# Strassen's products for half of h in two more chunks, and bursts of small matmuls moved by empty TensorE instructions

## The chip, the cores and the metric

The kernel runs on one NeuronCore of a Trainium2 chip. A core has TensorE (matmuls into PSUM), VectorE (DVE in the profile), ScalarE (ACT), GpSimd (POOL), SyncE (SP) and 16 DMA engines. The metric is the device time of one execution in microseconds, the median of several. The profile's span runs from the first to the last instruction of the program and is a little shorter than that time.

## The reference

Eight batches of eight heads pass through a linear attention with cosine weights; its output goes, token by token, through a two-layer network with a swish whose slope is a vector.

```python
# q, k, v: (8, 8, 576, 64); w_in: (512, 2048); w_out: (2048, 512); beta: (2048,)
q_p = concat(relu(q) * cos, relu(q) * sin)          # the same for k
kv  = einsum('bhsf,bhsd->bhfd', k_p, v)
z   = sum(k_p, axis=2)
num = einsum('bhsf,bhfd->bhsd', q_p, kv)
den = einsum('bhsf,bhf->bhs', q_p, z) + 1e-6
x   = num / den                                     # 4608 tokens x 512
h   = x @ w_in
out = (h * sigmoid(beta * h)) @ w_out               # 4608 x 512, float32
```

## The kernel before

The 4608 tokens are cut into nine chunks of 512 (c = 0 to 8). While chunk c passes through the network, the attention of batch b = c + 1 is done between its matmuls. All matmuls of the network are bfloat16.

**The first layer.** h of a chunk is 16 row tiles (jt) of 128 x 512. The plain way takes four matmuls of 128x512 for a tile:

```python
def h_mm(c, jt, mis=range(4), blocks=slice(0, NB)):
    ...
        nc.tensor.matmul(ps[:, h_bank(c, jt), ...], lhsT=win[jt // 4][:, mi, ...], rhs=xt[:, blocks, jp, ...], ...)

def h_plain(c, jt, bank, cols=1):       # the same; cols=2 cuts three of the four matmuls into two of 128x256
    w = NB // cols
    for mi in range(MI):
        for o in range(0, NB, w) if mi else (0,):
            ...
            nc.tensor.matmul(ps[:, bank, o * 64 : z * 64], lhsT=win[...], rhs=xt[:, o:z, jp, ...], ...)
```

From chunk FAST = 5 on, eight of the 16 tiles are done in four pairs (named X, Y, Z, V) by Strassen's scheme in Winograd's form: a pair is a product of 2 x 2 blocks that takes seven block products instead of eight. Each block product is two matmuls of 128x256, so a pair takes 14 of 128x256 where the plain way takes eight of 128x512. The operands that are sums of blocks are made on VectorE: four of the weights for each pair, once for all chunks (`wh_sums`), and four of x in each chunk (`x_sums`, or `x_sum` one at a time).

```python
def wh_sums(jt):                        # four TENSOR_TENSORs of 128x256
    ...
def x_sums(c):                          # four TENSOR_TENSORs of 128x512, from the chunk's x
    ...
def h_fast(c, jt0, banks):
    ops = {
        "1": lambda: prod(b_ps, w(0, 0), x(0, 0), True, False),   # prod: two matmuls of 128x256
        "5": lambda: prod(e_ps, s1, t1, True, False),
        "6": lambda: prod(b_ps, s2, t2, False, False),
        "2": ...  "7": ...  "3": ...  "4": ...
        "c1": lambda: nc.scalar.copy(p1, b_ps),                   # copies and additions between the products
        "c5": lambda: nc.vector.tensor_copy(p5, e_ps),
        "cu": ...  "a2": ...  "a7": ...  "a3": ...
        "Sa": ...  "Sb": ...                                      # SiLU of the two tiles
    }
```

**The second layer.** From chunk 2 on it is wholly done by the same scheme, in two halves x and y: seven products each, every one of eight matmuls of 128x256 (`o_fast`). Its sums over g (`g_sums`, tiles S1 to S4) are made on VectorE while h is computed. `cols` can cut a product's matmuls into two of 128x128.

**The attention.** Two groups of small matmuls of a batch come in bursts, without anything between them: `kv_mm` (72 matmuls of 64x130) and `num_all` (3 x 48 = 144 matmuls of 64x65). With the weight loads, the second is a burst of 288 TensorE instructions. VectorE then divides (`x_div`: sum, reciprocal and product, for a third of the batch each), and a DMA transposes the result into a chunk's x.

**The order in chunks 2 to 4 (before FAST).** `h_first` runs the 16 tiles plainly and puts the sums of VectorE between them; then the burst and the second layer:

```python
def h_first(c):
    for slot in range(16):
        h_group(c, slot)
        if c == 2: ...                             # k, v and q of the next batch on VectorE
        if slot == (10 if c == 2 else 1):
            kv_all(b)
        if slot in (3, 7, 11):
            g_sums(c, slot // 2 - 1, slot // 2 + 1)
        elif slot in (13, 15):
            sums = g_sums(c, slot // 2, slot // 2 + 1)
        if c == FAST - 1 and slot in (2, 4, 6, 8, 10, 12):
            wh_sums((0, 4, 8, 12, 2, 6)[slot // 2 - 1])

parts = (6, 0, 4) if c < FAST else (0, 6, 4)       # PSUM banks of the burst's thirds
xb, yb = (2, 3, 6), ...                            # banks of the second layer: b, e, a
...
sums = h_first(c)
for t, bank in enumerate(parts):
    num_all(b, t, bank)                            # the burst
for i, n in enumerate("156273"):
    x[n]()                                         # products 1, 5, 6, 2, 7, 3; product 2 writes bank 6
    if n in "156":
        ...
        x_part(b, i, parts[i])                     # x_div and the transpose
...                                                # the half y, with v of the next batch between
if c == FAST - 1:
    x_sums(c + 1)                                  # behind all v_half of VectorE
```

**From FAST on** one string gives the order of all operations: p0 to p7 are plain tiles, sp their SiLU, X5 a product of pair X, a2X an addition, s13 a sum of g, K and N the two bursts, ox5 a product of the second layer, v, w, k, q the next batch's preparation, t1 to t4 the sums of x for the next chunk. ORDER serves chunks 5 and 6, ORDER_END chunks 7 and 8. Two tables, H_COLS and O_COLS, cut matmuls of chunks 5 and 6 in two.

Of the kernel before, what the change touches and what calls it, by code (L numbers as in the profile page):

```python
# [22 lines left out]
def kernel(  # L23
# [172 lines left out]
    def q_relu(b, jp, eng="dve"):  # L196
        relu(qb[:, jp].rearrange("q n (j d) -> q j n d", j=2), raw_tile(b, "q")[:, 2 * jp : 2 * jp + 2], eng)
# [130 lines left out]
    def num_all(b, t, bank):  # L328
        for i in range(3):
            for jp in range(2):  # L330
                num_mm(b, 3 * t + i, jp, bank, 2 * i + jp)
# [82 lines left out]
    def h_silu(c, jt, bank):  # L414
        if (c, jt // 4) not in gs:
            gs[c, jt // 4] = gt_pool.tile([P, 4, TCH], BF16, name="g_t", tag="g_t")
        nc.scalar.activation(gs[c, jt // 4][:, jt % 4], ps[:, bank], AF.Silu, scale=beta[:, jt : jt + 1])  # L417

    def h_plain(c, jt, bank, cols=1):
        xt = xt_tile(c)  # L420
        w = NB // cols
        for mi in range(MI):
            jp, g = divmod(mi, 2)
            for o in range(0, NB, w) if mi else (0,):
                z = o + w if mi else NB
                nc.tensor.matmul(ps[:, bank, o * 64 : z * 64], lhsT=win[jt // 4][:, mi, (jt % 4) * P : (jt % 4 + 1) * P],  # L426
                                 rhs=xt[:, o:z, jp, g * HP : (g + 1) * HP],
                                 start=(mi == 0), stop=(mi == MI - 1 and z == NB))
# [101 lines left out]
    def o_part(c, tt, part, cols=1):  # L530
        o_mm(c, tt, range(4 * part, 4 * part + 4), cols)
# [226 lines left out]
    def v_half(b, cs, n0=0, n1=NQ, eng="dve"):  # L758
        if b >= B:
            return  # L760
        v_scale(b, cs, n0=n0, n1=n1, eng=eng)
        if cs == 1 and n1 == NQ and b + 1 < B:
            load_raw(b + 1, "v")
# [65 lines left out]
    for slot in range(32):  # L829
        if slot < 16:  # L830
            h_group(1, slot)
        else:
            o_part(1, (slot - 16) // 4, slot % 4, 2 if slot > 23 else 1)
        one_unit(slot)

    def k_piece(b, j):
# [4 lines left out]
            load_raw(b + 1, "k")  # L841

    ORDER = (
        "Y1 c1Y X5 X1 c5X c1X p0 X6 Y6 cuX X2 cuY X3 a2X a3X sp0 K X7 p1 kt Z1 Y5 a7X c5Y X4 SaX sp1 SbX "
        "Y7 a7Y s01 p2 Y2 s03 Z5 a2Y c1Z sp2 Y4 Y3 SbY Z6 Z2 a3Y SaY p4 V5 a2Z c5Z cuZ s02 c5V V1 p3 q0 "
        "sp4 Z7 V3 c1V V2 V6 a7Z Z3 sp3 Z4 cuV q1 p5 a3Z a2V SbZ V7 SaZ s11 s04 a3V a7V p6 sp5 s12 p7 "
        "sp6 s13 SaV V4 s21 s23 s14 SbV s22 N0 sp7 ox1 s31 ox5 s32 k1 x0 c1o s33 ox6 k0 k2 k3 c5o oy1 "
        "s24 ox2 s34 g0 g1 v8 w4 v4 x1 c1y o2x ox3 v2 v7 cuo x2 oy6 ox7 oy2 cuy o3x o7x oy5 oy7 ox4 w8 "
        "o2y v6 c5y t1 t3 oy3 w1 w0 o7y t2 v5 v3 oy4 t4 o3y w7 v1 w6 c4x w5 w3 w2 v0 c4y")
    ORDER_END = (  # L850
        "E1 F1 E2 X1 c1E X5 c1X X2 E5 a2E c5X X6 E6 X3 c1F a2X Y1 cuX X7 c5E cuE c1Y E3 E7 Y6 a3X SaX cuY "
        "a7X a3E Y5 SaE a7E X4 F6 F5 Y7 c5Y E4 Y2 cuF c5F Y3 F7 F2 a7Y a3Y a7F SbX SbE Y4 F3 a2Y Z1 a2F "
# [1 line left out]
        "V2 sp4 s13 sp5 V7 Z7 p6 a2V a3V s12 SaZ p7 SaV a7V sp6 sp7 a7Z s02 Z4 s14 V4 s04 oy1 SbV s31 SbZ "  # L854
        "s21 c1y s22 ox1 ox2 s32 t1 c1o ox5 o2x s34 s24 oy6 ox6 cuy cuo s23 oy2 s33 oy7 c5o ox3 ox7 o3x "
        "o7x oy5 c5y ox4 c4x t2 o7y oy3 t4 t3 o2y o3y oy4 c4y")
    H_COLS, O_COLS = {6: 8}, {5: ("4", "25734")}

    def x_sum(c, kind):
        xt, n = xt_tile(c), NB // 2  # L860
# [5 lines left out]
    def prep(b, left):  # L866

        def take(op):
            n = int(op[1])
            if op[0] in "kvw" and b + 1 < B:  # L870
                if op[0] == "k":
                    k_relu(b + 1, n, n + 1, "act")
                else:
                    v_scale(b + 1, "wv".index(op[0]), n0=n, n1=n + 1, eng="act" if op[0] == "v" else "dve")
            elif op[0] == "q" and b + 2 < B:
                q_relu(b + 2, n)
            for names, act in left:
                if names and op in names:
                    names.discard(op)
                    if not names:  # L880
                        act()

        return take

    def chunk(c, b, x, y, parts):
        steady = {"X": (0, 2, 0, 1), "Y": (4, 3, 4, 5), "Z": (8, 0, 2, 1), "V": (12, 4, 3, 5)}
        end = {"X": (0, 6, 0, 1), "E": (2, 5, 3, 4), "Y": (4, 2, 0, 1), "F": (6, 7, 3, 4), "Z": (8, 6, 0, 1),
               "V": (12, 5, 3, 4)}
        pairs = {n: h_fast(c, at[0], at[1:]) for n, at in (steady if b < B else end).items()}

        def plain_bank(n):
            return (2 if n == 7 else 6 + n % 2) if b < B else (2, 7)[n % 2]

        plain = [2, 3, 6, 7, 10, 11, 14, 15]
        outs = {"x": x, "y": y}

        def q_next():
            if b + 2 < B:
                q_turn_dma(b + 2)
                if b + 3 < B:  # L900
                    load_raw(b + 3, "q")

        def raw_next(name):
            if b + 2 < B:
                load_raw(b + 2, name)

        xs_all = {"x0", "x1", "x2"}
        take = prep(b, [
            ({"k0", "k1", "k2", "k3"} | xs_all, lambda: raw_next("k")),
            ({"q0", "q1"} | xs_all, q_next),  # L910
            ({f"{o}{n}" for o in "vw" for n in range(NQ)}, lambda: raw_next("v"))])
        last_sum = None
        for op in (ORDER if b < B else ORDER_END).split():
            n = int(op[-1]) if op[-1].isdigit() else None
            if op == "K":
                kv_mm(b, 0, 4)
                kv_mm(b, 1, 4)
            elif op == "kt":
                kv_take((0, 1), 4)
            elif op[0] == "N":  # L920
                for t, bank in enumerate(parts):
                    num_all(b, t, bank)
            elif op[0] == "x":
                x_part(b, n, parts[n])
                take(op)
            elif op[0] in "kvwq":
                take(op)
            elif op[0] == "t":
                if c + 1 < NTC:
                    x_sum(c + 1, n)  # L930
            elif op[0] == "g":
                if b + 1 < B:
                    q_tan(b + 1, n, None if n else last_sum)
            elif op[0] == "p":
                h_plain(c, plain[n], plain_bank(n), 2 if n < H_COLS.get(c, 0) else 1)
            elif op[:2] == "sp":
                h_silu(c, plain[n], plain_bank(n))
            elif op[0] == "o" and n is not None:
                outs[op[1]][op[2]]()
            elif op[0] == "o":  # L940
                outs[op[2]]["a" + op[1]]()
            elif op[0] == "c" and op[2] in "xyo":
                outs["x" if op[2] == "o" else op[2]][op[:2]]()
            elif op[0] == "s":
                last_sum = g_sum(c, 2 * int(op[1]), 2 * int(op[1]) + 2, n)
            else:
                pair = op[0] if op[0] in pairs else op[-1]
                pairs[pair][op.replace(pair, "")]()

    def h_first(c):  # L950
        b = c + 1
        for slot in range(16):
            h_group(c, slot)
            if c == 2:
                if slot == 0:
                    wx_tiles()
                    k_all(b)
                    v_half(b, 1)
                if slot == 3:
                    att_q(b + 1)  # L960
                if slot == 5:
                    nc.vector.tensor_tensor(T3, B22, B12, op=ALU.subtract)
# [3 lines that stand above are left out]
                g_sums(c, slot // 2 - 1, slot // 2 + 1)  # L966
            elif slot in (13, 15):
                sums = g_sums(c, slot // 2, slot // 2 + 1)
            if c == FAST - 1 and slot in (2, 4, 6, 8, 10, 12):
                wh_sums((0, 4, 8, 12, 2, 6)[slot // 2 - 1])  # L970
        return sums

    FAST = 5
    for c in range(2, NTC):
        b = c + 1
        parts = (6, 0, 4) if c < FAST else (0, 6, 4)
        cols = O_COLS.get(c, ("", ""))
        xb, yb = ((2, 3, 6), (1 if c == FAST - 1 else 7, 3, 6)) if c < FAST else ((3, 2, 0), (1, 2, 0)) if b < B else ((0, 3, 6), (1, 3, 6))
        x, y = o_fast(c, 0, xb, cols[0]), o_fast(c, 1, yb, cols[1])
        if c >= FAST:  # L980
            chunk(c, b, x, y, parts)
            continue
        sums = h_first(c)
        for t, bank in enumerate(parts):
            num_all(b, t, bank)
        q_tan(b + 1, 0, sums)
        q_tan(b + 1, 1)
        for i, n in enumerate("156273"):
# [12 lines left out]
        x["4"]()  # L1001
        x["c4"]()
        v_half(b + 1, 1, 1, 2, "act")
        v_half(b + 1, 0, 0, 3)
        y["5"]()
        y["c5"]()
        v_half(b + 1, 1, 2, 3, "act")
        y["6"]()
        y["cu"]()
        y["2"]()  # L1010
        y["a2"]()
        v_half(b + 1, 0, 3, 5)
        y["7"]()
        y["a7"]()
        v_half(b + 1, 0, 5, 7)
        y["3"]()
        y["a3"]()
        v_half(b + 1, 0, 7, 9)
        if c == FAST - 1:
            x_sums(c + 1)  # L1020
        v_half(b + 1, 1, 3, 9, "act")
        y["4"]()
        y["c4"]()
# [30 lines left out]
```

## Time and profile before

| | |
|---|---|
| time, median of 3 runs | 282.03 us (281.68 to 282.23) |
| span of the profiled run | 279.6 us |
| TensorE, matmuls busy | 272.2 us, 97% of the span |
| VectorE busy | 209.1 us, 75% |
| ScalarE busy | 177.8 us, 64% |
| GpSimd busy | 71.9 us, 26% |
| TensorE's clock | 1.0 in the whole span |

A busy share is the part of the span in which an engine had an instruction in work. Matmuls are pipelined, and the profile shows each with its latency, so the busy time of one group is not a number of matmuls times the mean of one; how fast a stream of them runs is read from the chain of work that ended last, which lists stretches of equal matmuls with their counts. "Issue" is idle time of an engine for which the profile shows nothing that was waited for.

### The profile page before, as it was taken

To read this page: it belongs to the slowest core of one execution; us is meant where nothing else is said; L and a number is where in the kernel's file an instruction comes from. 1 tells how busy PE (TensorE), PEld (TensorE's weight loads), DVE (VectorE), ACT (ScalarE), POOL (GpSimd) and SP (SyncE) were. 2 spreads that over 40 slices of the span, in tenths; PEclk is the share of its full clock that TensorE was granted. 3 is DMA by queue.
4 is the path that set the end of the run, shared out by engine and by line. 5 is a ranking of instruction groups with operands and counts; after the bars stand their busy time and mean duration, and the time that the engine had idled before them with its cause. 6 is when DMAs were issued, how large, how long until landed. Compare 5 with 4: busy or idle time off the path is not lost.

```text
span 279.6 us, 8687 instructions
## 1 busy us (share of the span) xinstructions
PE 272.2 (97%) x3592; PEld 192.4 (69%) x3592; DVE 209.1 (75%) x539; ACT 177.8 (64%) x348; POOL 71.9 (26%) x89
## 2 busy tenths in 40 slices
PE   8999999999999999999999999999999999999993
PEld 8564455455674588548854886679888886888783
DVE  5989967669999586357749977799679779649832
ACT  5778756772137557675757585896685179529911
POOL 1444000633194074106320542007400140000000
PEclk9999999999999999999999999999999999999999
DMA  7999999999979959992899289407400540033006
GB/s 243 373 394 385 391 390 323 348 244 397 164 233 330 293 151 249 182 340 41 196 193 374 61 205 250 177 12 115 116 1 7 122 113 1 2 79 74 0 2 150
DMA packets 50583, 53.98 MB, mean 193 GB/s; under 512 B 31200, under 2 KB 31472, under 8 KB 50544
## 3 DMA queue, kind: packets, MB, share of 16 engines
q1 hardware_dynamic: 47584, 45.82, 58.0%
q0 software_dynamic: 2688, 7.34, 9.2%
q8 instruction: 28, 0.46, 0.7%
q10 hardware_dynamic: 272, 0.27, 0.4%
q14 instruction: 11, 0.09, 0.2%
HBM read 36.71 MB, written 9.44 MB: 165 GB/s over the span
## 4 chain that ended last, share of the span: by engine, by line
PE 89%; DMA 5%; DVE 3%; issue 1%; ACT 0%; ACTq 0%
PE ps L544 30%; PE ps L378 22%; PE ps L472 11%; PE ps L521 8%; PE ps L426 7%; DMA raw_q<-in_q_dram 5%; PE ps L293 4%; PE ps L272 3%; PE ps L602 1%; PE ps L234 1%; PE ps L606 1%; DVE xs L315 1%; DVE vb L219 0%; PE ps L616 0%; PE ps L352 0%
## 5 line engine op out<-in xcount | busy, mean ns | idle before, releaser
L378 PE MATMUL ps<-xt,win 128*128 128x512 bf16 (+1 forms) x324 | 71.1, 377 | 0.1
L386 ACT ACTIVATE g_t<-ps,beta 128x512 bf16<-128x512 f32 x80 | 54.6, 688 | 19.2 <-PE ps L378 17.9
L378 PEld LDWEIGHTS <-win 128*128 128x128 bf16 x324 | 31.1, 98 | 35.4 <-issue 0.2
L514 POOL DMA_DIRECT2D out_dram<-o_sb x56 | 32.7, 590 | 66.6 <-DVE o_sb L595 34.3
L544 PEld LDWEIGHTS <-S 128*128 128x128 bf16 x469 | 44.2, 98 | 4.8
L417 ACT ACTIVATE g_t<-ps,beta 128x512 bf16<-128x512 f32 x64 | 41.2, 696 | 3.4 <-PE ps L426 2.2
L544 PEld LDWEIGHTS <-g_t 128*128 128x128 bf16 x357 | 32.9, 98 | 3.7
L222 POOL TENSOR_TENSOR qs<-qt,tanr 128x1152 bf16<-128x1152 bf16 x8 | 18.9, 2387 | 48.5 <-DVE S L397 17.6
L397 DVE TENSOR_TENSOR S<-g_t 128x512 bf16<-128x512 bf16 (+1 forms) x62 | 22.3, 393 | 11.5 <-ACT g_t L386 9.1
L521 PE MATMUL ps<-wout,g_t 128*128 128x512 bf16 (+1 forms) x158 | 29.2, 339 | 0.0
L544 PE MATMUL ps<-wout,g_t 128*128 128x256 bf16 (+1 forms) x231 | 28.1, 270 | 0.0
L544 PE MATMUL ps<-wout,S 128*128 128x256 bf16 (+1 forms) x238 | 27.4, 266 | 0.0
L544 PE MATMUL ps<-T,S 128*128 128x256 bf16 (+1 forms) x231 | 27.1, 269 | 0.0
L426 PE MATMUL ps<-xt,win 128*128 128x512 bf16 (+1 forms) x120 | 24.0, 336 | 0.0
L315 DVE TENSOR_TENSOR xs<-ps,rden 128x768 bf16<-128x768 f32 (+4 forms) x26 | 22.8, 883 | 0.8
L219 DVE TENSOR_SCALAR vb<-raw_v,cos 128x256 bf16<-128x256 f32 x63 | 22.9, 421 | 0.2 <-DMA raw_v<-in_v_dram 0.2
L521 PEld LDWEIGHTS <-g_t 128*128 128x128 bf16 x158 | 15.0, 98 | 11.0
L217 ACT ACTIVATE vb<-raw_v,sin 128x256 bf16<-128x256 f32 (+1 forms) x50 | 21.8, 499 | 0.8 <-DMA raw_v<-in_v_dram 0.8
L472 PE MATMUL ps<-w_stage 128*128 128x256 bf16 x120 | 20.3, 273 | 0.4 <-DVE w_stage L458 0.4
L472 PEld LDWEIGHTS <-w_stage 128*128 128x128 bf16 x160 | 15.5, 98 | 4.2 <-issue 0.5
L222 POOL TENSOR_TENSOR w_stage<-qt,tanr 128x1152 bf16<-128x1152 bf16 x4 | 9.5, 2380 | 26.1 <-DVE den L304 26.1
L426 PEld LDWEIGHTS <-win 128*128 128x128 bf16 x120 | 11.7, 98 | 6.3
(104 smaller groups left out, 384.9 us busy)
## 6 DMA issues: line engine op xcount, KB each, us to landing
raw_v<-in_v_dram SPq DMA_DIRECT2D x7, 1152.0 KB, 10.9
raw_k<-in_k_dram SPq DMA_DIRECT2D x7, 1152.0 KB, 8.4
raw_q<-in_q_dram SPq DMA_DIRECT2D x7, 1152.0 KB, 7.8
out_dram<-o_sb POOLq DMA_DIRECT2D x56, 128.0 KB, 5.2
w_stage<-in_moe_w_in_dram SPq DMA_DIRECT2D x3, 1024.0 KB, 13.3
w_stage<-in_moe_w_out_dram SPq DMA_DIRECT2D x2, 1024.0 KB, 8.4
w_stage<-in_moe_w_out_dram SPq DMA_DIRECT2D x4, 512.0 KB, 12.0
out_dram<-o_sb SPq DMA_DIRECT2D x13, 128.0 KB, 2.4
```

The source lines that it names most:

```text
L219: nc.vector.tensor_scalar(o, a, scalar1=t[:, n : n + 1], scalar2=None, op0=ALU.mult)
L222: return eng.tensor_tensor(dst.rearrange("q n (g p) -> q n g p", g=2), src.rearrange("q n (g p) -> q n g p", g=2), tanr[:, n0:n1].unsqueez ...
L315: nc.vector.tensor_tensor(o.rearrange("q j n s d -> q j (n s) d"), nv[:, :, a:z, :, 0:D].rearrange("q j n s d -> q j (n s) d"), rden[:, :, ...
L378: nc.tensor.matmul(ps[:, h_bank(c, jt), blocks.start * 64 : blocks.stop * 64], lhsT=win[jt // 4][:, mi, (jt % 4) * P : (jt % 4 + 1) * P], ...
L386: nc.scalar.activation(gs[c, jt // 4][:, jt % 4], ps[:, h_bank(c, jt)], AF.Silu, scale=beta[:, jt : jt + 1])
L397: return nc.vector.tensor_tensor(o, l, r, op=op)
L417: nc.scalar.activation(gs[c, jt // 4][:, jt % 4], ps[:, bank], AF.Silu, scale=beta[:, jt : jt + 1])
L426: nc.tensor.matmul(ps[:, bank, o * 64 : z * 64], lhsT=win[jt // 4][:, mi, (jt % 4) * P : (jt % 4 + 1) * P], rhs=xt[:, o:z, jp, g * HP : (g ...
L472: nc.tensor.matmul(dst, lhsT=left[:, g], rhs=right[:, :, g * HP : (g + 1) * HP], start=start and g == 0, stop=stop and g == 1, skip_group_ ...
L514: eng.dma_start(out=out_v[bb, n][:, m0:m1], in_=o_sb[hf * HP : (hf + 1) * HP, m0:m1])
L521: nc.tensor.matmul(o_ps[:, m0 : m0 + w], lhsT=gs[c, jt // 4][:, jt % 4, tt * P : (tt + 1) * P], rhs=wout[:, jt, m0 : m0 + w], start=(jt == ...
L544: nc.tensor.matmul(dst[:, m : m + w], lhsT=left(i), rhs=right[:, i, m : m + w], start=start and i == 0, stop=stop and i == order[-1], skip ...
```

## The change

Chunks 3 and 4 go over to the order of ORDER and so to Strassen's products for half of h (FAST from 5 to 3). ORDER itself is another order of the same operations. The sums of the weights move to chunk 2, those for the last two chunks into chunk 6. The cuts of H_COLS and O_COLS go; in chunk 1 five more groups of the second layer have their matmuls cut. In their place `pad` puts empty instructions (nops) on TensorE: PADS gives for a chunk how many at its start and how many behind its burst of 144 matmuls. They compute nothing and shift the place of the bursts in TensorE's stream of instructions.

```diff
+    def pad(c, n):
+        for _ in range(PADS.get(c, (0, 0))[n]):
+            nc.tensor.nop(hint="pad", nofuse=True)
@@ chunk 1
-            o_part(1, (slot - 16) // 4, slot % 4, 2 if slot > 23 else 1)
+            o_part(1, (slot - 16) // 4, slot % 4, 2 if slot > 18 else 1)
@@ the order
-        "Y1 c1Y X5 X1 c5X c1X p0 X6 Y6 cuX X2 cuY X3 a2X a3X sp0 K X7 p1 kt ... c4y")
+        "p0 Y1 X1 c1X p1 X5 c5X sp0 X6 X2 K c1Y X3 cuX kt Y6 X7 p2 a2X a3X ... ox4 ... oy2 ... oy4 w6 t2 v1 c4y v0 o2y w2 t4")
...
-    H_COLS, O_COLS = {6: 8}, {5: ("4", "25734")}
+    PADS = {2: (35, 9), 3: (144, 42), 4: (153, 38), 5: (143, 0)}
@@ inside a chunk of ORDER
+            elif op[0] == "q" and b + 1 == B:
+                wh_sums((2, 6)[n])
...
                     num_all(b, t, bank)
+                pad(c, 1)
...
-                h_plain(c, plain[n], plain_bank(n), 2 if n < H_COLS.get(c, 0) else 1)
+                h_plain(c, plain[n], plain_bank(n))
@@ h_first
-            if c == FAST - 1 and slot in (2, 4, 6, 8, 10, 12):
-                wh_sums((0, 4, 8, 12, 2, 6)[slot // 2 - 1])
+            if slot in (10, 12, 14):
+                for jt in ((0, 4), (8,), (12,))[slot // 2 - 5]:
+                    wh_sums(jt)
@@ the chunks
-    FAST = 5
+    FAST = 3
     for c in range(2, NTC):
...
-        cols = O_COLS.get(c, ("", ""))
+        pad(c, 0)
...
-        x, y = o_fast(c, 0, xb, cols[0]), o_fast(c, 1, yb, cols[1])
+        x, y = o_fast(c, 0, xb), o_fast(c, 1, yb)
...
         for t, bank in enumerate(parts):
             num_all(b, t, bank)
+        pad(c, 1)
...
-        v_half(b + 1, 0, 0, 3)
+        v_half(b + 1, 0, 0, 5)
         y["5"]()
         y["c5"]()
+        if c == FAST - 1:
+            x_sums(c + 1)
...
-        v_half(b + 1, 0, 3, 5)
...
-        if c == FAST - 1:
-            x_sums(c + 1)
```

## The prediction

> **What bounds the kernel now.** I read the page's busy times first, then the chain of work that ended last, then the timeline around every place where that chain leaves TensorE's matmuls.
>
> ```profile
> PE 272.2 (97%) x3592; PEld 192.4 (69%) x3592; DVE 209.1 (75%) x539; ACT 177.8 (64%) x348; POOL 71.9 (26%) x89
> PE 89%; DMA 5%; DVE 3%; issue 1%; ACT 0%; ACTq 0%
> q8 instruction: 28, 0.46, 0.7%
> ```
>
> TensorE has a matmul in work for 97% of the span and carries 89% of the chain; the DMA and DVE shares lie in the start-up (the 5% is one load up to 39 us, beside which TensorE is busy). So from chunk 2 on time is saved by giving TensorE fewer columns to stream or fewer stops, and by nothing else. The third line returns below. The chain of chunks 2 and 3, the two that pay something avoidable, in order of time (start, length, what):
>
> ```profile
> 91.89 4.42 PE ps L378 x20
> 96.31 1.33 PE ps L293 x132
> 97.64 0.43 issue
> 98.06 0.23 PE ps L293 x4
> 98.29 12.33 PE ps L544 x112
> 110.62 1.73 PE ps L378 x8
> 112.35 1.15 PE ps L272 x72
> 113.49 12.19 PE ps L378 x56
> 125.69 1.25 PE ps L293 x124
> 126.94 0.48 issue
> 127.42 0.29 PE ps L293 x13
> 127.71 2.29 PE ps L544 x20
> ```
>
> First the price of a matmul: 56 of 128x512 in 12.19 us are 0.217 us each, 112 of 128x256 in 12.33 us are 0.110 us. The half-width one costs almost exactly half; chunk 5's cut products give 0.056 us for 128x128 in the same way (154 matmuls in 12.44 us, of which 70 are of 128x256). Second, the stops: both bursts of 144 small matmuls break off near their end, for a reason that no semaphore shows ("issue").
>
> ```profile
> 97.42 0.22 PE L293 MATMUL ps<-kv,qt 64*64 64x65 bf16 x4
> 98.06 0.23 PE L293 MATMUL ps<-kv,qs 64*64 64x65 bf16 x4 [0.43 <-issue]
> 127.42 0.19 PE L293 MATMUL ps<-kv,qt 64*64 64x65 bf16 x1 [0.48 <-issue]
> ```
>
> In the burst a group of four starts every 0.03 us; here the next comes 0.64 us after the last. From start to start the two stops cost 0.61 and 0.69 us, 1.3 us together. Going through all matmuls after 45 us and taking off the standard interval of each, only one more place loses over 0.2 us, 0.5 us at the start of chunk 5:
>
> ```profile
> 169.37 0.38 PE L472 MATMUL ps<-w_stage 128*128 128x256 bf16 x2 [0.35 <-DVE w_stage L458]
> ```
>
> A Strassen product waits there for a sum of x that VectorE made behind its v scaling.
>
> **What the Trainium skill says.** "Runtime: NRT & Kernel Launch", section Instruction fetch mechanics: an engine's instructions come through a FIFO that is refilled by DMA in 16 KiB blocks of 256 instructions. The trace agrees: 28 instruction packets of 0.46 MB are 16 KB each, and 7,189 TensorE instructions are 28 blocks. The section also holds that issue is slow enough to hide the fetch; in the burst it isn't: 288 instructions (weight loads and matmuls) pass in 1.43 us, 5 ns each, while the instruction packets take about 1.0 us apiece. The place of the stops fits: counted in the trace, they stand before TensorE instructions 2,753 and 3,521, which are 768 = 3 x 256 apart. The stopped bursts start 24 and 7 instructions before a multiple of that grid and so cross two borders, the second within 1.3 us of the first; those of chunks 1, 4, 5 and 6 cross one (after 237, 246, 181 and 240 instructions) and don't stop. "TensorE: Matmul & The Clock Gate", section Back-to-back issue gap, gives 262 and 518 cycles for 256 and 512 columns, 109 and 216 ns at 2.4 GHz; the trace has 110 and 217. "PSUM — Partial Sum Buffer", section Engine vs sequencer instructions: a nop runs on the sequencer itself and isn't handed to the engine's queue. No run shows what one costs there.
>
> **The change part by part.**
>
> *Columns.* From the list of TensorE's instructions before and after: 490 to 431 matmuls of 128x512, 1,138 to 1,282 of 128x256, 156 to 72 of 128x128. By the prices above: -59 x 0.217 = -12.8; +144 x 0.110 = +15.8; -84 x 0.056 = -4.7. Sum -1.7 us, all on the path. Strassen is worth (32 x 0.217 - 56 x 0.110) = 0.8 us a chunk; the cuts removed or added are nearly free, as two halves cost what the whole does.
>
> *Bursts.* Counting the changed list in the same way (nops included), the bursts of chunks 2 to 6 start so that the first border comes after 207, 245, 241, 251 and 186 of their 288 instructions: one border each. If the grid is the cause, both stops go: -1.3 us.
>
> *The sum of x at the old FAST.* x_sums moves ahead of four v scalings, and the new order begins a chunk with a plain tile, so the 0.5 us at 169 us should go: -0.5 us.
>
> *VectorE in chunk 2.* Four groups of weight sums move into slots 10 to 14, ahead of the last sums of g. A chain of four such operations takes 0.94 us (the four 128x256 sums of g, 97.07 to 98.01 in the timeline), so four groups are 3.8 us. VectorE ends kv at 92.6 and has about 1.9 us of waits from there to 98.0; the groups fill these and push the end of the g sums to about 99.7. x_div follows, 1.4 us for its first third (98.01 to 99.43 before), ending at about 101.2. Product 2 of half x writes bank 6, which that third reads. TensorE, rid of the burst's stop, reaches it at 97.6 + 24 x 0.109 = 100.2. It waits about 1.0 us; before it had 1.4 us to spare. +0.9 us.
>
> *Chunks 3 and 4.* VectorE gets 16 additions and copies of about 0.43 us and four sums of x of 0.42 us for each chunk, 8.6 us, ScalarE eight copies. Chunk 5 carries the same load before, with VectorE busy 3.1 to 4.8 us of every 5, and no stop inside it. I count nothing.
>
> *Nops, 564 of them.* Up to 153 at a chunk's start and up to 42 behind a burst. TensorE's sequencer runs ahead of the array: at the starts of chunks 1 to 5, 11 to 27 instructions were still unstarted when its semaphore instruction there ran, that is 0.6 to 1.5 us at 0.055 us each (half of 0.110, as each matmul has its weight load). Passed like the burst's instructions, in 5 ns, 150 nops are 0.75 us, mostly hidden; the 42 behind a burst are 0.2 us with little lead left. I count +0.4 us for all.
>
> Sum: 282.0 - 1.7 - 1.3 - 0.5 + 0.9 + 0.4 = 279.8 us.
>
> **The rivals.**
>
> *Costly nops.* The semaphore instructions of TensorE's sequencer take 51 ns each in the trace. If a nop takes as long, 144 need 7.3 us, of which at most 1.5 us is hidden: nearly 6 us lost at each of three chunk starts, about 2 us behind two bursts: 300 us or more. At 20 ns it is about 1.5 us a chunk start and 0.7 us behind a burst, some 6 us, and the time is 285 us. For it: nops are the sequencer's own work. Against it: the counts look tuned chunk by chunk, and a stop could be avoided by moving a burst at most 32 places, so nobody would put 144 there if each cost 50 ns.
>
> *A new wait in place of the old.* VectorE in chunk 2 as above, or the same in chunks 3 and 4: then 281 to 282 us. For it: VectorE has no gap from 76 to 90 us. Against it: later chunks run the same load freely.
>
> *Stops that aren't the grid's.* If they come from a crowded DMA, moving the bursts does nothing, and 281 us stay. Against it: the two stops are exactly three blocks apart.
>
> *All goes well.* No wait in chunk 2, nops free: 278.5 us. Over 2% would need 276.4; TensorE's columns don't allow it.
>
> **Range and chances.** The gains on TensorE are countable, 3.5 us at most. Nearly all the uncertainty is the price of a nop, and it goes one way. 279.8 us, eight times in ten between 278.3 and 284.5. Faster by over 2%: 0.04. Within 2%: 0.84. Slower by over 2% (above 287.7): 0.12.
>
> **What would show it.** The chain after has stretches of 112 matmuls at 12.3 us, chunks 3 and 4 about 0.8 us shorter by their first layer, and no "issue" inside a burst. Before product 2 of chunk 2 (a matmul of the second layer near 100 us) stands an idle of about 1 us released by VectorE's product of x_div. At the starts of chunks 3 to 5 TensorE's idle is under 0.3 us; several microseconds there, with nops or "issue" beside them, make the first rival right and this prediction wrong. A stop left inside a burst makes the grid wrong.

## The result, and the profile after

The changed kernel takes 322.74 us (median of 6 runs, 322.11 to 327.28) where the kernel before takes 282.10: a ratio of 1.146, with an interval of 1.141 to 1.150. I had predicted 279.8 us, within 278.3 to 284.5. The prediction was wrong by 43 us, and nearly all of that is one term of its sum: the nops.

The page of the changed kernel, in the lines shown before: the busy times, the granted clock of TensorE in 40 slices of the span, the instruction packets, and the chain by engine.

```profile
PE 277.0 (86%) x3587; PEld 196.8 (61%) x3593; DVE 219.7 (69%) x571; ACT 179.6 (56%) x364; POOL 71.7 (22%) x89
PEclk9999999999999987989859979679999999999998
q8 instruction: 30, 0.49, 0.6%
PE 66%; DVE 11%; issue 11%; DMA 10%; SPq 1%; ACTq 0%; ACT 0%; DVEq 0%
```

TensorE's share fell from 97 to 86%. Its busy time hardly grew, so the array stands idle for some 36 us more, and for the first time its clock drops in the middle of the kernel. The chain names VectorE and DMAs for a fifth of the span. That is not to be trusted here: behind an idle that has no semaphore to show, the chain follows whatever came last. The waits of TensorE's matmuls (engine and line, what it waited for, total us, times, longest) are plainer:

```profile
PE ps L430 <- issue: 27.4, 3, 9.5
PE ps L548 <- issue: 6.1, 3, 3.0
```

Line 430 is the plain tile at the start of a chunk of ORDER, line 548 the second layer behind the burst: the two places where the change puts its nops. In the chain, in order of time (start, length, what), around the first of them and behind the burst of the same chunk:

```profile
101.95 9.77 PE ps L548 x88
111.72 9.51 issue
121.23 1.87 PE ps L430 x4
...
136.98 1.38 PE ps L293 x133
138.35 2.97 issue
141.32 13.88 PE ps L548 x112
```

Between the second layer of chunk 2 and the first tile of chunk 3 nothing runs for 9.5 us. And the four matmuls that follow take 1.87 us, 0.47 each where 0.217 is usual; the 112 behind the burst take 13.88 and not 12.33. What stands in the gap is shown by the instructions of line 421, the nops (count, then min/median/max ns of one, then first and last start in us), here in six of their seven places:

```profile
L421 PEldq NOP  x35: 13/13/13, 79.1 to 81.8; - x35
L421 PEldq NOP  x144: 13/13/13, 110.6 to 121.0; - x144
L421 PEldq NOP  x42: 13/13/13, 138.2 to 141.3; - x42
L421 PEldq NOP  x153: 13/13/13, 153.2 to 164.3; - x153
L421 PEldq NOP  x38: 13/13/13, 182.1 to 184.8; - x38
L421 PEldq NOP  x143: 13/13/13, 196.9 to 207.4; - x143
```

A nop is recorded with 13 ns, and it is easy to stop reading there. But 144 of them start between 110.6 and 121.0 us: one every 0.073 us. The starts of single nops in a block are mostly 71 ns apart.

**The account.** Idle is counted from start to start of matmuls, less the standard interval.

| part | predicted, us | measured, us |
|---|---|---|
| columns of TensorE | -1.7 | -1.7 (worked out, same prices) |
| two stops inside bursts | -1.3 | -1.3 (gone) |
| sum of x at the old FAST | -0.5 | -0.5 (gone) |
| VectorE in chunk 2 | +0.9 | +0.4 |
| nops at chunk starts (0.91 + 9.68 + 9.46 + 8.80) | +0.4 for all | +28.9 |
| nops behind bursts (0.59 + 3.15 + 2.88, less 0.11 each that a burst's end costs anyway) | | +6.3 |
| matmuls at half the clock | 0 | +8.7 |
| sum | -2.2 | +40.8 |

The span grew from 279.6 to 320.3 us, by 40.7. The clock's part is read from the granted clock of four stretches of chunk 3 (from and to, length, TensorE's busy time and matmuls, granted clock, DMA share, GB/s):

```profile
121.20:123.60 2.40, 2.37 (x8) 0.50 1.04 387
123.90:136.00 12.10, 12.10 (x149) 1.00 0.07 22
141.30:144.30 3.00, 2.98 (x15) 0.50 0.51 99
144.50:153.00 8.50, 8.50 (x80) 1.00 0.36 68
```

In the clock's record the stretch at half begins before such an idle has ended or just behind it, and 2.7 to 5.1 us of matmuls fall into it. In the same record the stretches at half last 3.41, 6.83 or 10.24 us, one, two or three times 3.41. The Trainium skill ("TensorE: Matmul & The Clock Gate", section What's actually happening) describes just this: a gate that falls to half the pulses after an idle window of about 3.4 us and opens after a busy one. The idle that is enough for it was shorter here (3.15 us behind the burst of chunk 3), and shorter still in the experiments.

### The profile page after: what moved, and what is told of

The parts are those of the page before. It is cut to its first block, busy times and chain, and to the rows that moved or that the text cites. A ratio compares the mean times of both kernels' runs of the same rounds, so it can differ in the third digit from the quotient of the medians.

```text
span 320.3 us, 9276 instructions
## 1 busy us (share of the span) xinstructions
PE 277.0 (86%) x3587; PEld 196.8 (61%) x3593; DVE 219.7 (69%) x571; ACT 179.6 (56%) x364; POOL 71.7 (22%) x89
## 4 chain that ended last, share of the span: by engine, by line
PE 66%; DVE 11%; issue 11%; DMA 10%; SPq 1%; ACTq 0%; ACT 0%; DVEq 0%
PE ps L548 24%; PE ps L476 14%; PE ps L430 12%; PE ps L378 8%; DMA raw_q<-in_q_dram 5%; DMA raw_v<-in_v_dram 3%; DMA raw_k<-in_k_dram 3%; PE ps L293 2%; PE ps L525 2%; PE ps L272 2%; DVE xs L315 2%; DVE vb L219 2%; DVE T L407 1%; DVE S L397 1%; DVE qb L194 1%
## 5 line engine op out<-in xcount | busy, mean ns | idle before, releaser
L430 PE MATMUL ps<-xt,win 128*128 128x512 bf16 x160 | 44.9, 409 | 27.4 <-issue 27.4
L378 PE MATMUL ps<-xt,win 128*128 128x512 bf16 (+1 forms) x196 | 42.8, 375 | 0.8 <-DVE vb L219 0.7
L430 PEld LDWEIGHTS <-win 128*128 128x128 bf16 x160 | 16.3, 103 | 40.9 <-issue 31.1
L502 DVE COPY p<-ps 128x256 f32<-128x256 f32 x28 | 11.7, 417 | 40.3 <-PE ps L476 40.1
L548 PE MATMUL ps<-wout,g_t 128*128 128x256 bf16 x224 | 28.9, 280 | 6.3 <-issue 6.1
L378 PEld LDWEIGHTS <-win 128*128 128x128 bf16 x196 | 18.6, 98 | 22.1 <-issue 1.5
L501 ACT COPY p<-ps 128x256 f32<-128x256 f32 x28 | 10.3, 374 | 34.8 <-issue 21.9
L548 PE MATMUL ps<-T,S 128*128 128x256 bf16 x224 | 28.8, 285 | 0.0
L548 PE MATMUL ps<-wout,S 128*128 128x256 bf16 x224 | 27.4, 273 | 0.0
L476 PEld LDWEIGHTS <-w_stage 128*128 128x128 bf16 x224 | 21.8, 99 | 8.6 <-issue 0.8
L476 PE MATMUL ps<-w_stage 128*128 128x256 bf16 x168 | 27.0, 276 | 0.0
```

The source lines that it names most:

```text
L378: nc.tensor.matmul(ps[:, h_bank(c, jt), blocks.start * 64 : blocks.stop * 64], lhsT=win[jt // 4][:, mi, (jt % 4) * P : (jt % 4 + 1) * P], ...
L476: nc.tensor.matmul(dst, lhsT=left[:, g], rhs=right[:, :, g * HP : (g + 1) * HP], start=start and g == 0, stop=stop and g == 1, skip_group_ ...
L548: nc.tensor.matmul(dst[:, m : m + w], lhsT=left(i), rhs=right[:, i, m : m + w], start=start and i == 0, stop=stop and i == order[-1], skip ...
```

## The experiments

Theory A: TensorE's sequencer takes 0.071 to 0.073 us to pass a nop and hands nothing to the array meanwhile. Only the instructions that it has handed over before keep the array going. Rivals: B, the new order or VectorE's load holds chunks 3 to 5 up and the nops only stand beside it; B2, a nop costs the array time wherever it stands. A place in the stream is told as in the prediction, by how many of a burst's 288 instructions come before its first border of the grid of 256.

**e1: no nops.**

```diff
-    PADS = {2: (35, 9), 3: (144, 42), 4: (153, 38), 5: (143, 0)}
+    PADS = {}
```

> The changed kernel with an empty PADS table: no nop at all, everything else as in the change. Theory A (the sequencer spends 0.071 us on each nop and the array runs dry): all of the loss goes, and my sum without its nop term holds: 282.1 - 1.7 - 1.3 - 0.5 + 0.9 = 279.5 us, between 278.5 and 280.5. No burst crosses two borders of the grid here (the first border comes after 242, 177, 112, 47 and 238 instructions in chunks 2 to 6), so no burst breaks off. Before product 2 of chunk 2 about 0.9 us of idle released by VectorE's x_div. Theory B (the new order or the load of VectorE holds chunks 3 to 5 up, the nops only stand beside it): still above 290 us, with idle at the chunk starts.

Measured: 280.50 us, ratio to before 0.9955 (0.9931 to 0.9979). The whole loss goes with the nops, and B falls. The chunk starts have no idle (110.90 below is the first tile of chunk 3). The wait in chunk 2 is there, in the chain and in the timeline:

```profile
100.12 0.97 DVE xs L315
101.09 0.04 issue
101.13 9.77 PE ps L548 x88
110.90 0.86 PE ps L430 x4
```

```profile
101.13 0.60 PE L548 MATMUL ps<-wout,g_t 128*128 128x256 bf16 x4 [0.67 <-DVE xs L315]
184.98 0.27 PE L548 MATMUL ps<-wout,g_t 128*128 128x256 bf16 x1 [1.59 <-issue]
```

VectorE's product of x_div ends at 101.09, and product 2 of the second layer starts with it: 0.83 us from start to start against 0.9 predicted. The second line I had not expected: in chunk 5 TensorE stops again for 1.75 us, not inside the burst but before the eighth matmul behind it. This burst meets a border after 47 instructions, and the next border lies 15 instructions behind its end.

With this run the account closes without nops. Its span is 1.0 us shorter than before (278.7 and 279.6), and -1.7 for the columns, -1.3, -0.5, +0.83 and +1.75 make -0.9. That is the only test of the -1.7, which no single stretch shows.

**e2: the same 564 nops, spread.**

```diff
+    def drip(most):
+        for _ in range(min(most, owed[0])):
+            nc.tensor.nop(hint="pad", nofuse=True)
+            owed[0] -= 1
...
     (behind every matmul of the second layer and of the Strassen products)
+                drip(1)
     (behind every plain matmul of h)
+                drip(2)
```

> All 564 nops stay, but each stands alone behind one matmul of the second layer or of h (at most one behind a 128x256, two behind a 128x512) instead of in blocks; the bursts of 144 matmuls keep the places in the stream that they have in the change. Theory A: a nop and its pair of weight load and matmul take the sequencer about 0.08 us, less than the 0.109 us that the array needs for the pair, so the nops are hidden: within 0.5 us of the run without nops. Theory B2 (a nop costs the array time wherever it stands, by draining it or in another way): the 564 nops cost what they cost in the change, about 40 us; 315 us or more.

Measured: 285.09 us, ratio 1.0112 (1.0081 to 1.0143). B2 falls: the nops that cost 40 us in blocks cost less than 5 us one by one. But "within 0.5 us of the run without" is missed as well. The second layer shows what the nops themselves cost; with a nop behind nearly each matmul it runs as fast as ever, and the next burst breaks off:

```profile
101.47 9.77 PE ps L558 x88
...
125.50 1.21 PE ps L293 x113
126.71 2.84 issue
129.55 0.40 PE ps L293 x22
```

88 matmuls take 9.77 us with nops and without (e1 above); the nops among them start mostly 0.091 us apart, and the array needs 0.109 us for a pair. The loss is in the bursts: stops of 0.43, 0.30, 3.02 and 0.85 us in chunks 1 to 4, 4.6 us in all, and about 1.7 us at half the clock behind the longest; e1's stop of 1.75 us is absent. That makes 4.5 us, about the whole difference (4.6 us between the medians, 4.2 between the profiled spans). Whether the nops have a part in these stops is not shown: no nop stands ahead of the burst of chunk 1, and in chunks 2 to 4 the last one starts 13, 9.5 and 4.6 us before the burst. What the stops share is told below, under "Where the stops end".

**e3: 36 nops at each of three chunk starts.**

```diff
+    PADS = {3: (36, 0), 4: (36, 0), 5: (36, 0)}
```

> 36 nops in a block at the start of chunks 3, 4 and 5, none elsewhere. Theory A: 36 x 0.0735 = 2.6 us of the sequencer each, of which about 0.9 us is hidden by its lead: 1.7 us of idle at each start, 5.2 us together over the run without nops, so about 284.7 us; the idle is shorter than the 3 us and more after which the clock was seen halved, so the clock stays 1.0. If the loss were proportional (41 us for 564), it would be 7.8 us, 287 us, and the clock would fall too.

Measured: 286.12 us, ratio 1.0153 (1.0115 to 1.0191). The idle at the three starts is 1.90, 0.86 and 0.86 us, 3.6 us and not 5.2: I had set the lead of chunk 3 for all three. The lead comes out the same from both doses. 36 nops take 2.8 us at chunk 3, less 1.90 leaves 0.9; 144 take 10.6 us, less 9.68 leaves 0.9 (the change). At chunk 4, 36 x 0.0727 - 0.86 and 153 x 0.0733 - 9.46 both leave 1.76 us. So the loss is not proportional: the first 1.8 us of nops are free (0.9 us at chunk 3), all others cost their full 0.073 us. The lead can also be counted. When the first nop starts, 33 of the weight loads and matmuls ahead of it have not started yet, at chunks 2, 4 and 5 of the change and at 4 and 5 here; at chunk 3 it is 17 in both runs. There the first matmul of the last product waits for an addition of VectorE, and in the change the first nop follows the end of that addition by 0.06 us. "The clock stays 1.0" failed, for a reason that isn't the nops':

```profile
157.70 0.54 PE ps L548 x4
158.24 2.20 issue
160.44 4.78 PE ps L548 x28
```

The shift had put chunk 4's burst at 40, and the next border, 8 instructions behind it, stopped TensorE for 2.36 us; the clock went to half right there, for 3.41 us. The idle of 1.90 us at the start of chunk 3 left it alone.

**e4 and e7: the kernel before, with its bursts moved.** In e4, 36 nops are spread behind matmuls of 128x512 in chunk 2; in e7 194 more follow between the bursts of chunks 3 and 4, so that other bursts cross two borders.

```diff
+        owed[0] += {2: 36}.get(c, 0)
         sums = h_first(c)
         for t, bank in enumerate(parts):
             num_all(b, t, bank)
+        owed[0] += {3: 0}.get(c, 0)        # e7: {3: 194}
```

> The kernel before with 36 nops, at most two behind each of the first 18 matmuls of 128x512 in chunk 2, where the sequencer has time for them. They shift all later bursts by 36 places: the first border now comes after 244, 227, 210, 145 and 204 instructions in chunks 2 to 6, so no burst crosses two. If the grid of 256 instructions makes the stops, both go and the time falls by 1.3 us to 280.8 us. If the stops have another cause (a crowded DMA, the banks of PSUM), they stay at 97.4 and 126.7 us and the time is that of before.

> The kernel before with 36 nops spread behind matmuls of chunk 2 as in e4_before_36, and 194 more spread behind the second layer of chunk 3 and the first matmuls of chunk 4. The first border then comes after 244 and 227 instructions in chunks 2 and 3 and after 16, 207 and 10 in chunks 4, 5 and 6. If the grid makes the stops, they turn up where there were none, in chunks 4 and 6, and are gone from 2 and 3: two stops of 0.6 to 0.7 us, so 281.7 us again. If not, chunks 4 and 6 run on as before and the time is 280.4 us.

Measured: e4 280.42 us, ratio 0.9949 (0.9931 to 0.9968); e7 280.70 us, ratio 0.9993 (0.9976 to 1.0009). In e4 the stop of chunk 3 is gone and that of chunk 2 is 0.3 us long and not 0.6:

```profile
97.57 0.12 issue
97.69 0.38 PE ps L293 x22
98.08 12.33 PE ps L552 x112
...
125.47 1.36 PE ps L293 x135
126.83 4.26 PE ps L552 x38
```

In the profiled execution of e7 (282.28 us, long for this run) the stops of chunks 2 and 3 are gone, and chunk 4, which had none before, has one of 1.32 us:

```profile
157.09 0.22 PE L293 MATMUL ps<-kv,qt 64*64 64x65 bf16 x4 [1.13 <-issue]
```

Chunk 6, placed at 10, runs through; I had expected a stop there. So moving a burst moves its stop, but two borders in a burst don't always make one.

**Where the stops end.** The trace also has the instruction packets. For every stop of over 0.5 us in a burst or just behind it, before and in e1 to e7, the last packet's start and the first matmul or weight load after the stop:

| run, chunk | stop, us | packet starts | goes on at | between |
|---|---|---|---|---|
| before, 2 | 0.61 | 95.50 | 98.06 | 2.56 |
| before, 3 | 0.69 | 125.01 | 127.42 | 2.41 |
| e1, 5 | 1.75 | 182.56 | 184.98 | 2.42 |
| e2, 3 | 3.02 | 126.92 | 129.55 | 2.63 |
| e2, 4 | 0.85 | 157.38 | 160.01 | 2.63 |
| e3, 4 | 2.36 | 158.04 | 160.44 | 2.40 |
| e7, 4 | 1.32 | 154.53 | 157.09 | 2.56 |

The run e8 (below) has one more, of 1.29 us in chunk 5, 2.37 us behind a packet's start. All seven of the table stand before an instruction of the same place in the grid of 256 (counted in the trace, e7 with six records missing), and all end 2.4 to 2.6 us after the packet's start, although the packet itself takes about 1 us. A block of instructions can be used that long after its transfer began, and a stop is what is missing of it when the sequencer gets there.

**e5, e6: bursts placed by cut matmuls, and VectorE's load moved.**

```diff
     (e5, in the second layer, without nops)
+        cols = {4: ("4", "25734")}.get(c, ("", ""))
+        x, y = o_fast(c, 0, xb, cols[0]), o_fast(c, 1, yb, cols[1])
     (e6, besides: chunk 2 keeps the weight sums of two pairs, chunk 1 makes the other two)
-                for jt in ((0, 4), (8,), (12,))[slot // 2 - 5]:
-                    wh_sums(jt)
+                wh_sums(0); wh_sums(4)               # slot 10
...
+        elif slot == 9:                              # chunk 1
+            wx_tiles(); wh_sums(8); wh_sums(12)
```

> No nops, and 42 matmuls of chunk 4's second layer (products 4 of x, 2, 5, 7, 3 and 4 of y) cut into two of 128x128, as the kernel before did in chunk 5: 84 more instructions, which move the burst of chunk 5 so that its first border comes after 219 instructions and not 47 (chunk 6: 154 and not 238). Without nops one stop of 1.75 us was left, in chunk 5, 15 instructions behind the burst: its burst crosses one border near its start, and the next border comes right behind it, before the block that was asked for at the first is there. If that is its cause, it goes, and the cuts cost 0.1 us: 280.5 - 1.75 + 0.1 = 278.9 us. If it was the second layer's own wait (a sum of g, a bank), it stays and the time is 280.6 us.

> As e5_placed, and the weight sums of pairs Z and V are made in chunk 1, where VectorE waits 3.1 us for the products of kv, and not between the last sums of g of chunk 2. If VectorE's load is what holds product 2 of chunk 2 up by 0.7 to 0.8 us, that idle goes: 278.1 us, 1.3 to 1.4% under the kernel before. If the wait has another cause it stays: 278.9 us.

Measured: e5 279.00 us, ratio 0.9924 (0.9906 to 0.9943); the stop of chunk 5 is gone. e6 278.25 us, ratio 0.9897 (0.9875 to 0.9918); its second layer follows the burst of chunk 2 without a break:

```profile
96.39 1.36 PE ps L293 x135
97.76 12.33 PE ps L548 x112
110.09 0.86 PE ps L430 x4
```

So VectorE's load was the cause of that wait. e6 takes 1% less than the kernel before. Measured twice more, with the expectations below, it gave 278.91 us, 0.9904 (0.9874 to 0.9933), and 279.68 us, 0.9916 (0.9881 to 0.9950).

> e6_best once more on the same chip, so that e9_best_24 has its own comparison: 278.2 us.

> e6_best a third time, for the comparison with e11_roomy on one chip: 278.3 to 279.0 us, a stop at the end of the burst of chunk 2 in some runs.

The profiles of these repeats have a stop at the end of chunk 2's burst, 1.75 and 0.98 us, that the first profile lacks. Position and program are the same; the packet started at 96.74 and 96.13 us instead of 94.84. The traces show what stands beside it. In all profiles, before and after included, the packet of this place starts within half a microsecond of the end of a dense run of 256-byte DMA packets (about 113 in 0.1 us), and the transpose of q into qt is the only one issued in the 12 us before it. The run ends at 95.0 us in e6, at 97.0 in e10 and at 96.5 in e12. So in chunk 2 the packet is late when this transpose is late. No run moved the transpose, so that it holds the packet back is not shown; beside the longer stops of chunks 3 to 5 no such run was found at the packet's start.

**e8: the old order in chunks 3 to 6.**

```diff
-    ORDER = ( ... the new string ... )
+    ORDER = ( ... the string of the kernel before ... )
```

> No nops, and the string ORDER of the kernel before (for chunks 3 to 6), everything else as in the change. The count of instructions is the same, so the bursts stand at the same places and the stop of chunk 5 stays. If the new order matters little on its own: 280.5 us as without nops. If it was made to take a wait away: more, with an idle of 0.5 us at the start of chunk 3, where the old order wants a sum of x at once.

Measured: 298.92 us, ratio 1.0586 (1.0532 to 1.0640). The loss is far over both expectations (the stop of chunk 5 stays, as said). VectorE's waits and one moment of the timeline show why:

```profile
DVE qb L194 <- DMA raw_q<-in_q_dram: 17.0, 4, 7.8
```

```profile
127.73 0.76 DVE L194 TENSOR_SCALAR qb<-raw_q 128x1152 bf16<-128x1152 f32 x1 [7.08 <-DMA raw_q<-in_q_dram]
128.40 0.42 DVE L505 TENSOR_TENSOR ps<-ps,p 128x256 f32<-128x256 f32 x1
128.88 0.58 PE L476 MATMUL ps<-w_stage,win 128*128 128x256 bf16 x2 [6.59 <-DVE ps L505]
```

The old string has the relu of q (q0) in the first third of the chunk. In chunks 3 and 4 q isn't loaded by then. VectorE waits 7 us for it, behind it stands an addition of a Strassen pair, and behind that TensorE. The two stops of TensorE, in chunks 3 and 4, lose 6.7 and 7.5 us, and the half clock at them 4.5 us: 18.7 us, where the run takes 18.4 longer than e1. The new string has q0 and q1 near the end. That q0 alone makes the difference was not tested. But the new order is not a refinement: without it the kernel with Strassen's products in chunks 3 and 4 is 17.6 us slower than before.

**e9: 24 nops at two starts of e6.**

```diff
+    PADS = {4: (24, 0), 5: (24, 0)}
```

> e6_best with a block of 24 nops at the starts of chunks 4 and 5. The accounts of the change and of e3_36_each give the sequencer's lead there: 153 nops at 0.0733 us less 9.46 us of idle, and 36 at 0.0727 less 0.86 us, both leave 1.76 us hidden, which is 24 nops. If that lead is what hides nops, these 48 cost nothing: 278.2 us, idle under 0.1 us at both starts. If each nop costs its 0.072 us, 3.5 us more: 281.7 us.

Measured: 280.23 us, ratio 0.9948 (0.9931 to 0.9966). At chunk 4 the 24 nops cost nothing, as expected. At chunk 5 they cost 0.93 us:

```profile
138.01 1.03 PE L430 MATMUL ps<-xt,win 128*128 128x512 bf16 x4
...
168.06 0.81 PE L430 MATMUL ps<-xt,win 128*128 128x512 bf16 x3 [0.77 <-issue]
```

The matmuls ahead of chunk 5 are the cut ones here, of 128x128 with 0.056 us each. A lead of 1.76 us at 0.055 us an instruction is 32 instructions; at 0.028 us 32 are 0.9 us, and 24 nops less that leave the 0.9 us seen. Counted in the trace, 33 are unstarted here too at the first nop. The lead is a count of instructions, not a time. The profile has a further loss, a stop of 1.0 us in chunk 4, at the border 56 instructions behind the burst (placed at 88). e10, its comparison on the same chip, takes 278.91 us.

**e11: all bursts with room on both sides.** As e6, with more cut matmuls in chunks 1, 3, 4, 5 and 6.

```diff
-            o_part(1, (slot - 16) // 4, slot % 4, 2 if slot > 18 else 1)
+            o_part(1, (slot - 16) // 4, slot % 4, 2)
-        cols = {4: ("4", "25734")}.get(c, ("", ""))
+        cols = {3: ("4", "25734"), 5: ("4", "25734")}.get(c, ("", ""))
-                h_plain(c, plain[n], plain_bank(n))
+                h_plain(c, plain[n], plain_bank(n), 2 if c in (4, 6) else 1)
```

> e6_best with more cuts and no nops, so that the bursts of chunks 2 to 6 meet their first border after 220, 155, 214, 149 and 208 instructions: in e6_best it was 242 in chunk 2, only 14 instructions after the border before it, and one of its two profiles showed a stop of 1.75 us there, where the fetch began 2 us later than in the other. If a stop needs two borders within about 2.5 us of each other, none of these bursts has one, now or at another time: 278.4 us (the cuts cost 0.3 us) and less spread than the 278.2 to 280.5 of e10_best_again. If stops come from the load of the DMA alone, one is still seen in some runs and the spread stays.

Measured: 281.73 us, 279.87 to 284.76, ratio 1.0001 (0.9973 to 1.0029); e12 beside it took 279.68. The expectation failed. The profile, of an execution of 284.49 us, near the top of the range, has stops of 1.87 and 1.93 us at the borders inside the bursts of chunks 2 and 4, placed at 220 and 214, again 2.4 and 2.7 us behind a packet's start. The packets started after the bursts had begun, though the border before lies 36 and 42 instructions ahead of them. Room in the stream is not enough; what delays the start of a packet was not tested and stays open. The page also shows the clock:

```profile
PEclk9999999999999999999999799999999999999999
```

The one 7 is a stretch of 3.41 us at half the clock, 1.2 us behind the stop of 1.93 us in chunk 4. The stop of 1.87 us in chunk 2 has none. In the change, too, the stretches at half begin whole multiples of 3.41 us apart (117.11, 141.00, 158.07, 185.38, 202.44 us), so it may count how an idle falls into these periods; that was not tested.

## Why the prediction was wrong, point by point

**The step that failed** is "Passed like the burst's instructions, in 5 ns, 150 nops are 0.75 us, mostly hidden ... I count +0.4 us for all". A nop takes the sequencer 0.071 us, fourteen times that; the blocks cost 28.9 + 6.3 us of idle and 8.7 us at half the clock, 43.9 us in place of 0.4. The sign that it had set for this, several microseconds of idle at the starts of chunks 3 to 5, came: 9.68, 9.46 and 8.80. It had come near the price: its first rival took the 51 ns of the sequencer's semaphore instructions and came to "300 us or more". I set it aside because "nobody would put 144 there if each cost 50 ns". That is a reason about the author, not about the chip, and it was worth nothing. Even the rival was too small: 51 ns is the recorded duration, and a nop's recorded 13 ns shows how little of an instruction's time on the sequencer that is; the clock was not in it at all.

**The lead** ("0.6 to 1.5 us") was nearly right: 0.9 us at chunk 3, 1.76 us at 4 and 5, next to nothing behind a burst, of whose instructions 0 to 7 were unstarted at the first nop.

**Columns, stops, sum of x**: the change shows the last two gone, and the span of e1 fits all three. Without the nop term the prediction's sum is 279.4 us; e1, without nops, takes 280.5 with a stop of 1.75 us more than I had counted.

**VectorE in chunk 2**: right in mechanism and size, 0.83 us in e1 against 0.9. In the change only 0.4 us were left, as the nops at the start of chunk 2 and behind its burst made TensorE late for it.

**Chunks 3 and 4, "I count nothing"**: right for the new order, and for a reason that the prediction didn't see: with the old one e8 is 17.6 us slower than the kernel before.

**The grid**: right that the stops stand on it, too simple as a rule. A burst that crosses one border near its start can stop behind its end (e1, e3, e9), and one that ran through in one execution can stop in another, when its packet is late (e6 against e10 and e12). "Stops that aren't the grid's ... a crowded DMA" was dismissed too quickly: the grid says where a stop can be, the packet's start whether and how long.

## What to carry to other kernels

An instruction that computes nothing still passes the sequencer: price it from the spacing of its kind, not from its recorded duration, and compare the block with the lead that the engine has at that place, counted in instructions. If a stream must be shifted, cut a matmul in two, or set single nops between matmuls that are longer than a nop with its pair (0.091 against 0.109 us here). Neither is safe against new stops: 36 single nops gained 1.5 us (e4) where 564 lost 4.6 (e2 against e1), and one set of cuts helped (e5) where another did not (e11). Where an order of operations is new, look first at what stands in it behind a DMA on an engine that works in order.

## What the runs showed of the hardware that was not expected

- A nop on TensorE is recorded with 13 ns and takes 71 ns from one to the next; in the burst weight loads and matmuls pass at 5 ns each.
- TensorE's sequencer is about 33 instructions ahead where nothing holds it up (1.76 us behind matmuls of 128x256, 0.9 us behind matmuls of 128x128).
- A block of 256 instructions was usable 2.4 to 2.7 us after its packet's transfer began, in all thirteen stops of over 0.5 us at the borders, before and in e1 to e12; the transfer takes about 1 us.
- Idles of 2.36 us (e3) and 1.93 us (e11) were enough for the clock to be halved for 3.41 us; idles of 1.90 us (e3), 1.87 us (e11) and 1.75 us (e1) were not. The length of the idle alone gives no threshold that a run here has shown.
